# Raw weight loads behind the second pair's keys and queries, and one filler product per bank

## Chip, cores and metric

The kernel runs on one core of a Trainium2 chip. The metric is the device time of one execution in microseconds (us), as the median of several runs.

## What is computed

Causal attention with a decay per key (4 batches, 8 heads, 576 positions, head size 64), then a feed-forward layer with a maximum of three products, then a second one with a rational gate.

```python
def _attn_ref(q, k, v, f):
    scores = (1.0 / np.sqrt(D)) * np.matmul(q, k.transpose(0, 1, 3, 2))
    cum = np.cumsum(np.log(np.clip(f, 0.0001, 1.0)), axis=-1)
    scores = np.where(causal, -1e9, scores + cum[:, :, :, None] - cum[:, :, None, :])
    attn = softmax(scores)                       # row maximum subtracted
    return np.matmul(attn, v)

def _moe_ref(x, w1, w2, w3, w_out):              # 2304 x 512, d_ff 768
    h = np.maximum(np.maximum(x @ w1, x @ w2), x @ w3)
    return h @ w_out

def _moe2_ref(x, w_in, w_out, a, b):             # 2304 x 512, d_ff 2048
    h = x @ w_in
    P = a[0] + a[1]*h + a[2]*h**2 + a[3]*h**3
    Q = 1.0 + abs(b[0])*abs(h) + abs(b[1])*h**2
    return (P / (Q + 1e-6)) @ w_out
```

The weights of the two layers arrive as 64-bit floats; everything else is 32-bit.

## The kernel before

**Pairs, units and steps.** Attention works on pairs of heads (class Pair) and on units, one head of a pair with one group of query blocks (class Unit). Group 0 has the first 320 positions (three blocks), group 1 the other 256 (two blocks). The first batch comes as eight pairs: pairs 0 to 3 with group 0, pairs 4 to 7 with group 1. Later batches have both groups in one pair. A loop over steps (from L596) does, for three units at once, the last part of one (attend), the transposes of the next (turn), and the scores of a third, and prepares a pair some steps before its first unit.

**A pair's way.** load puts keys (kn) and queries (qn) into memory by three transfers each (L269, L272); both use a two-buffer tag, so a pair's loads wait for the transposes of the pair before. prepare transposes the keys on TensorE (L334) and copies them out on ScalarE (L308, tile kf), then fetches the decay rows of the keys by small transfers (copies, L57: kf<-nch for pair 0, from the tile nch; kf<-ncd for the others, from a copy in DRAM), then does the queries (L334, L320). scores multiplies both (L385, in the first batch two instructions on TensorE per product), VectorE adds the mask and finds the row maximum (L389), ScalarE takes the exponential (L395), GpSimd normalises (L404), TensorE transposes (L424), ScalarE copies out (L426), and attend multiplies with the values (L440).

**Fillers.** exercised (L80) issues WARM products of the tile warm, 128x512 in the fp32r type (L84), into a bank of PSUM before the bank's real work writes it. Their results are overwritten. It does so for pairs 0 to 3 (n < 4): at the transposes of keys and queries, the scores, the transposed probabilities and the outputs. That is 52 banks, so 104 fillers.

**Weights.** A 64-bit weight tile is loaded raw (load_raw, L167, 512 KB for w1 to w3) and converted into a high and a low 32-bit part: ScalarE (L181), VectorE (L186, L187, L188, L191), ScalarE (L197), GpSimd (L200). The list conv holds 30 such conversions: 18 of w1, w2 and w3, 12 of w_out. ahead holds the raw loads of the first three; each conversion begun later also issues one raw load further on. Two conversions are begun before the steps, the rest by fill, at 0.15 for each call before step 7 and 0.5 after it. Raw loads keep the order of the program among themselves and stand on the queue of SP, as all loads do.

**Order.** A planner orders the instructions of each engine ahead of the run, by its own estimates of their durations and of the program's order. On the chip each engine and SP's queue then work strictly in that order.

Of the kernel before, what the change touches and what calls it, by code (L numbers as in the profile page):

```python
# [37 lines left out]
def kernel(  # L38
# [17 lines left out]
    def move(dst, src):  # L56
        return nc.sync.dma_start(r32(dst), r32(src))  # L57
# [22 lines left out]
    def exercised(bank, n):  # L80

        if n < 4:
            for _ in range(WARM):
                nc.tensor.matmul(bank, warm[:, 0], wide, start=True, stop=True)  # L84
        return bank

    WARM = 2
    mask = const.tile([P, S], F32, name="mask")
    nc.gpsimd.memset(mask, 0.0)
    nc.gpsimd.affine_select(  # L90
# [424 lines left out]
    pairs = [Pair(n, *j) for n, j in enumerate(jobs)]  # L515
# [12 lines left out]
    ahead = [load_ for load_, _ in conv[: LOOK + 1]]  # L528
# [50 lines left out]
        return NCONV - int(state["c"])  # L579

    pairs[0].load()
    for load_ in ahead:
        load_()
    LV = 1
    lvat = {}
    for p in pairs[1:]:
# [2 lines left out]
        f_()  # L589
    move(ncd, nch)  # L590
    pairs[0].load_v()
    for _ in range(2):
        conv.pop(0)()
    pairs[1].load()
    ab = const.tile([P, 8], F32, name="ab")
    for step in range(len(slots) + 2):  # L596
        u = slots[step] if step < len(slots) else None
# [257 lines left out]
```

## Time and profile before

| | before |
|---|---|
| median of three runs | 959.67 us (959.0 to 960.5) |
| profiled execution | 959.34 us |
| its span, first to last instruction | 957.5 us |
| TensorE (PE) busy | 934.7 us (98%) |
| VectorE (DVE) | 725.0 us (76%) |
| ScalarE (ACT) | 641.3 us (67%) |
| GpSimd (POOL) | 252.0 us (26%) |
| mean granted clock of TensorE | 0.99 |

Busy times are of one profiled execution. PEld is TensorE's weight load, beside its products; SPq is the issue of a transfer on SP's queue. A matmul's recorded duration overlaps the next one's, so distances between starts, or the chain that ended last, tell what one costs in a stream. The granted clock is given as a share of full speed.

### The profile page before, as it was taken

To read this page: it belongs to the slowest core of one execution; us is meant where nothing else is said; L and a number is where in the kernel's file an instruction comes from. 1 tells how busy PE (TensorE), PEld (TensorE's weight loads), DVE (VectorE), ACT (ScalarE), POOL (GpSimd) and SP (SyncE) were. 2 spreads that over 40 slices of the span, in tenths; PEclk is the share of its full clock that TensorE was granted. 3 is DMA by queue.
4 is the path that set the end of the run, shared out by engine and by line. 5 is a ranking of instruction groups with operands and counts; after the bars stand their busy time and mean duration, and the time that the engine had idled before them with its cause. 6 is when DMAs were issued, how large, how long until landed. Compare 5 with 4: busy or idle time off the path is not lost.

```text
span 957.5 us, 16833 instructions
## 1 busy us (share of the span) xinstructions
PE 934.7 (98%) x5780; PEld 828.5 (87%) x5780; DVE 725.0 (76%) x1692; ACT 641.3 (67%) x1526; POOL 252.0 (26%) x408
## 2 busy tenths in 40 slices
PE   7989999999999999999999999999999999999998
PEld 5757899998998989999999988888888888899997
DVE  7578875556776786534297969888988988899996
ACT  6786667777767676656454558667666666777765
POOL 3355654444554465424132400000000000000000
PEclk9997999999999999999999999999999999999999
DMA  5784223123555455220145477011002102100000
GB/s 160 201 227 124 82 75 85 43 65 97 145 160 173 136 175 152 71 91 1 62 137 180 141 256 272 1 45 44 1 1 66 44 1 66 44 1 1 34 1 34
DMA packets 125741, 88.52 MB, mean 92 GB/s; under 512 B 74572, under 2 KB 110424, under 8 KB 125656
## 3 DMA queue, kind: packets, MB, share of 16 engines
q1 hardware_dynamic: 125656, 87.45, 30.5%
q8 instruction: 46, 0.75, 0.3%
q14 instruction: 39, 0.32, 0.1%
HBM read 64.73 MB, written 22.69 MB: 91 GB/s over the span
## 4 chain that ended last, share of the span: by engine, by line
PE 81%; DVE 12%; ACT 2%; issue 2%; DMA 2%; SPq 0%; POOL 0%; ACTq 0%; DVEq 0%; POOLq 0%
PE hq L730 7%; PE hq L728 7%; PE oo L778 7%; PE oo L779 7%; PE hq L729 7%; PE oo L777 7%; PE h L472 6%; PE h L473 5%; PE h L474 5%; PE o L440 5%; PE tp L424 5%; PE x2p L498 2%; PE s L388 2%; PE x2p L500 2%; PE s L387 2%
## 5 line engine op out<-in xcount | busy, mean ns | idle before, releaser
L472 PE MATMUL h<-x,w1h 128*128 128x320 f32 (+1 forms) x576 | 177.0, 308 | 2.0 <-DVE m L480 1.4
L474 PE MATMUL h<-x,w1l 128*128 128x320 f32 (+1 forms) x576 | 172.3, 299 | 0.0
L473 PE MATMUL h<-x,w1h 128*128 128x320 f32 (+1 forms) x576 | 172.2, 299 | 0.0
L404 POOL TENSOR_SCALAR e<-e,rs 128x64 f32<-128x64 f32 (+4 forms) x160 | 89.2, 573 | 104.3 <-DVE rs L401 90.7
L472 PEld LDWEIGHTS h<-x,w1h 128*128 128x128 f32 x576 | 109.7, 190 | 4.8 <-DVE m L480 1.6
L778 PE MATMUL oo<-wp,gh 128*128 128x512 f32 x288 | 112.6, 391 | 0.0
L777 PE MATMUL oo<-wp,gh 128*128 128x512 f32 x288 | 112.0, 389 | 0.0
L395 ACT ACTIVATE e<-e,st 128x64 f32<-128x64 f32 (+4 forms) x160 | 88.9, 556 | 32.1 <-DVE st L389 30.6
L473 PEld LDWEIGHTS h<-x,w1h 128*128 128x128 f32 x576 | 109.8, 191 | 0.4 <-ACT w1h L197 0.2
L737 ACT ACTIVATE s<-hq 128x512 f32<-128x512 f32 (+1 forms) x80 | 44.3, 554 | 97.6 <-PE hq L730 97.5
L474 PEld LDWEIGHTS h<-x,w1l 128*128 128x128 f32 x576 | 109.6, 190 | 0.0
L779 PE MATMUL oo<-wp,gl 128*128 128x512 f32 x288 | 109.1, 391 | 0.0
L389 DVE CUSTOM_DVE_ANT_0 e<-s,mask 128x320 f32<-128x320 f32 (+3 forms) x160 | 67.3, 432 | 37.2 <-PE s L388 27.3
L426 ACT ACTIVATE pt<-tp 128x384 f32<-128x384 f32 (+3 forms) x160 | 70.2, 470 | 21.5 <-PE tp L424 18.4
L740 DVE SCALAR_TENSOR_TENSOR s<-s,ab,u 128x512 f32<-128x512 f32 (+1 forms) x80 | 55.7, 696 | 32.3 <-ACT u L738 32.2
L424 PE MATMUL tp<-ident,e 128*128 128x128 f32 (+1 forms) x480 | 78.5, 279 | 1.5 <-DVE k2s L312 1.1
L730 PE MATMUL hq<-x,wil 128*128 128x512 f32 (+1 forms) x192 | 69.9, 364 | 0.0
L728 PE MATMUL hq<-x,wih 128*128 128x512 f32 (+1 forms) x192 | 69.8, 363 | 0.0
L729 PE MATMUL hq<-x,wih 128*128 128x512 f32 (+1 forms) x192 | 69.7, 363 | 0.0
L779 PEld LDWEIGHTS oo<-wp,gl 128*128 128x128 f32 x288 | 54.0, 188 | 11.3
L778 PEld LDWEIGHTS oo<-wp,gh 128*128 128x128 f32 x288 | 54.0, 188 | 10.5
L777 PEld LDWEIGHTS oo<-wp,gh 128*128 128x128 f32 x288 | 54.1, 188 | 10.4
(132 smaller groups left out, 2425.1 us busy)
## 6 DMA issues: line engine op xcount, KB each, us to landing
raw_w<-in_moe_w_dram SPq DMA_DIRECT2D x18, 512.0 KB
raw_wp<-in_moe_w_out_dram SPq DMA_DIRECT2D x32, 256.0 KB
wpd<-wp SPq DMA_DIRECT2D x32, 256.0 KB
raw_wi<-in_moe_w_in_dram SPq DMA_DIRECT2D x32, 256.0 KB
wp<-wpd SPq DMA_DIRECT2D x10, 768.0 KB
x2d<-xo SPq DMA_DIRECT2D x16, 320.0 KB
out_dram<-ob SPq DMA_DIRECT2D x18, 256.0 KB
kn<-in_k_dram SPq DMA_DIRECT2D x32, 128.0 KB
```

Source lines behind the costliest of these rows:

```text
L395: nc.scalar.activation(e[:nr], e[:nr], AF.Exp, bias=m, scale=-1.0, accum_out=l)
L404: nc.gpsimd.tensor_scalar(e, e, self.rs[:, 1, j : j + 1], 0.0, op0=ALU.mult, op1=ALU.add)
L424: nc.tensor.transpose(tp[:kr, dst : dst + P], self.e[i][:, Q0[c] : Q1[c]], ident)
L472: nc.tensor.matmul(hp_[:, :w], wh[:, j, dc], xs[dc][:, 1], start=(dc == NDC - 1), stop=False)
L473: nc.tensor.matmul(hp_[:, :w], wh[:, j, dc], xs[dc][:, 0], start=False, stop=False)
L474: nc.tensor.matmul(hp_[:, :w], wl[:, j, dc], xs[dc][:, 0], start=False, stop=(dc == 0))
L728: nc.tensor.matmul(hp_[:, :w], wih[:, dc, fs], xh, start=(dc == 0), stop=False)
L729: nc.tensor.matmul(hp_[:, :w], wih[:, dc, fs], xl, start=False, stop=False)
L730: nc.tensor.matmul(hp_[:, :w], wil[:, dc, fs], xh, start=False, stop=(dc == NDC - 1))
L777: nc.tensor.matmul(o, g[0][:, ts_], wh_, start=(fc == 0), stop=False)
L778: nc.tensor.matmul(o, g[0][:, ts_], wl_, start=False, stop=False)
L779: nc.tensor.matmul(o, g[1][:, ts_], wh_, start=False, stop=(fc == NF2 - 1))
```

## The change

Two edits. WARM goes from 2 to 1, so each of the 52 banks gets one filler. The raw loads in ahead, and the first two conversions with the raw load that they issue, stand in the program behind pair 0's values and behind pair 1's keys and queries; before, ahead stood directly behind pair 0's loads, and the two conversions ahead of pair 1's.

```diff
-    WARM = 2
+    WARM = 1
...
     pairs[0].load()
-    for load_ in ahead:
-        load_()
     LV = 1
...
     move(ncd, nch)
     pairs[0].load_v()
+    pairs[1].load()
+    for load_ in ahead:
+        load_()
     for _ in range(2):
         conv.pop(0)()
-    pairs[1].load()
     ab = const.tile([P, 8], F32, name="ab")
```

## Rows read from the trace of the kernel before

**Rows 1.** The page, part 1: busy time, share of the span, instructions of each engine.
```profile
PE 934.7 (98%) x5780; PEld 828.5 (87%) x5780; DVE 725.0 (76%) x1692; ACT 641.3 (67%) x1526; POOL 252.0 (26%) x408
```

**Rows 2.** Table of stages: from:to, length, busy us (instructions) per engine, clock, DMA.
```profile
22.00:49.00 27.00, 27.00 (x159) 21.37 (x158) 14.22 (x53) 21.19 (x65) 11.23 (x20) 1.00 0.70 189
49.00:55.00 6.00, 6.00 (x41) 4.53 (x39) 1.89 (x10) 5.80 (x21) 3.77 (x6) 1.00 0.33 76
60.00:68.00 8.00, 5.03 (x26) 2.44 (x25) 7.96 (x17) 7.61 (x19) 3.81 (x4) 1.00 1.17 301
68.00:82.00 14.00, 11.36 (x39) 8.30 (x38) 13.19 (x26) 10.39 (x24) 10.01 (x9) 0.51 0.63 179
108.00:300.00 192.00, 189.59 (x1470) 174.13 (x1467) 124.59 (x413) 138.74 (x412) 96.36 (x172) 1.00 0.37 101
```

**Rows 3.** The chain that ended last, 0 to 30 us: start, us, what.
```profile
6.62 5.09 DMA kf<-nch
12.27 4.18 DMA kn<-in_k_dram
23.86 0.47 PE s L84 x2
26.49 0.33 PE tk L334 x3
```

**Rows 4.** Timeline, 0 to 40 us: start, us, engine, line, operation, tiles, [idle before].
```profile
0.75 0.40 SPq L103 DMA_DIRECT2D fl<-in_f_dram  x1
3.19 0.45 DVE L108 TENSOR_SCALAR fl<-fl 32x576 f32<-32x576 f32 x1
4.22 1.57 SPq L167 DMA_DIRECT2D raw_w<-in_moe_w_dram  x3
5.75 1.20 PE L84 MATMUL tq<-warm 128*128 128x512 f32 x2
5.90 2.50 SPq L57 DMA_DIRECT2D kf<-nch  x4
10.16 0.56 PE L334 MATMUL tq<-ident,qn 128*128 128x128 f32 x3
11.70 0.47 SPq L167 DMA_DIRECT2D raw_w<-in_moe_w_dram  x1
11.84 0.79 PE L385 MATMUL s<-kf,qf 66*128 66x64 f32 x4 [0.65 <-DMA kf<-nch]
12.27 0.45 SPq L269 DMA_DIRECT2D kn<-in_k_dram  x1
15.33 1.10 SPq L57 DMA_DIRECT2D kf<-ncd  x2
22.03 0.71 PE L385 MATMUL s<-kf,qf 66*128 66x64 f32 x4
```

**Rows 5.** SP's waits, 0 to 20 us: line, releaser, total us, times, longest.
```profile
SPq L272 <- DMA raw_w<-in_moe_w_dram: 1.3, 1, 1.3
```

**Rows 6.** Table of stretches of 2 us, columns as in rows 2, GB/s last.
```profile
8.00:10.00 2.00, 2.00 (x6) 1.55 (x5) 1.09 (x3) 1.03 (x2) 0.00 (x0) 1.00 1.08 363
18.00:20.00 2.00, 2.00 (x6) 1.31 (x6) 1.59 (x7) 1.07 (x3) 0.46 (x1) 0.50 0.30 68
```

**Rows 7.** Groups of a conversion's steps, 22 to 49 us: busy us, mean ns, idle before.
```profile
L181 ACT ACTIVATE cv_w<-raw_w 128x512 f32<-128x512 f32 x4 | 2.4, 659 | 0.0
L197 ACT ACTIVATE w1h<-cv_w 128x512 fp32r<-128x512 f32 x5 | 3.1, 624 | 1.4 <-DVE cv_w L191 1.4
L188 DVE SCALAR_TENSOR_TENSOR cv_w<-raw_w,cv_w 128x512 int32<-128x512 int32 x4 | 2.6, 680 | 0.0
```

**Rows 8.** TensorE from 22 to 49 us: lines L84, L424 and L334, in this order.
```profile
22.00:49.00 27.00, 19.98 (x59) 9.64 (x58) 1.00 0.70 189
22.00:49.00 27.00, 5.11 (x31) 3.66 (x32) 1.00 0.70 189
22.00:49.00 27.00, 2.33 (x15) 1.95 (x15) 1.00 0.70 189
```

## The prediction, made before the changed kernel ran

> **What bounds the kernel now.** Read the page's engine shares first: TensorE is busy 934.7 of 957.5 us [rows 1]. Nearly everything after 108 us is a full TensorE (189.59 of 192 us up to 300 us), so a gain has to come from the first 100 us and reach the end as a shift. The table by stages then says what each early stage is worth [rows 2]. From 22 to 49 us TensorE is busy 27.00 of 27 us at granted clock 1.00, while ScalarE has 21.19 and VectorE 14.22. From 49 to 55 us ScalarE is full beside it (5.80 of 6). From 60 to 68 us VectorE is the full engine (7.96 of 8) and TensorE has only 5.03. At the very start the chain that ended last runs through two transfers: 5.09 us for the first pair's decay rows (kf<-nch) and 4.18 us for the second pair's keys [rows 3]. The timeline shows why: three raw weight tiles of 512 KB leave SP at 4.22, ahead of the four decay rows (5.90 to 8.40), and a fourth at 11.70, just ahead of those keys (12.27) [rows 4].
>
> My sum is made against the profiled execution, 959.34 us (span 957.5 and 1.84 around it). The median of the runs is 959.67, so 0.33 is added at the end.
>
> **Edit 1, the raw weights: the first pair.** Without them the decay rows have an empty ring. The nearest row for a transfer with nothing ahead of it is fl: issue ends at 1.15, its reader starts at 3.19, so 2.0 us [rows 4]. The first head's two rows have left SP by about 7.15, all four by 8.40: they land at 9.2 to 10.4 instead of 11.71. The queries must also be there: their transposes stand at 10.16, behind ten fillers that take 5.75 to 10.16, 0.44 us each. Half of those and one of the two ahead of the key transposes go, 2.6 us; so they start near 7.55. The first scores stand 1.1 us behind the last of these transposes (10.72 to 11.84), for the copy between. First scores: 7.55 + 0.56 + 1.1, about 9.2 for 11.84, 2.6 us earlier.
>
> **The second pair's keys.** Two things leave SP ahead of them: the fourth raw weight (0.57 us from 11.70 to 12.27), and a wait of 1.3 us for a raw weight that stood inside the first values' issue [rows 5]. They leave at about 10.7, and the first block is there at 10.7 + 0.4 + 2.0 = 13.1 instead of 16.45: 3.3 us earlier. TensorE, in order, waits for them in both versions.
>
> **What it moves into the way.** The four raw weights now stand on SP ahead of the second pair's decay rows (kf<-ncd, 15.33 now), and ahead of every later key, query and value load. SP reaches them near 13.7 (10.7 and six loads of 0.5 us). Upper bound: before, rows behind three such tiles landed 7.5 us after the first tile's issue (4.22 to 11.71); a fourth adds 0.5 MB at 363 GB/s [rows 6], 1.45 us, so 13.7 + 9.0 = 22.7. Lower bound: four tiles at 363 GB/s need 5.9 us, so about 20. The second pair's scores started at 22.03 [rows 4]. Everything else they need would be ready 5.0 us earlier, at 17.0 (3.3 from the keys, and five of the ten fillers between 16.5 and 22 us, 1.7 at 0.34 each, midway between 0.23 and 0.44). So the wait that left the keys comes back at these rows, and most of the gain with it. Gain at this point: between 5.0 (if the planner puts the rows ahead of the weights, or other TensorE work into the hole) and -0.7. I take 0.7, near the end given by the row that shows just such a queue.
>
> The conversions of these weights start some 10 us later. On VectorE a conversion has four steps, none over L188's 0.68 us [rows 7], so at most 2.7 us, and 10.9 for four; it has 12.8 us free from 22 to 49 [rows 2]: covered, unless the planner puts a conversion whose weight hasn't landed ahead of a score (rival 2). GpSimd has 15.8 us free there: covered too. ScalarE pays 0.66 + 0.62 us per conversion [rows 7]; about two of the four now fall behind 22 us: 2.6 us.
>
> **Edit 2, the fillers.** From 22 to 49 us 59 records of L84 stand on TensorE [rows 8]. A pair takes 0.47 us of the chain [rows 3], 0.23 each; 30 fewer are 6.8 us. If nothing else bounded, the stage would be 20.2 us. But ScalarE has 21.19 us of its own and receives 2.6: 23.8 us. So 27.0 - 23.8 = 3.2 us are gained. Bounds: 0, if the chain of score, exponential, normalisation and transpose leaves ScalarE as many holes as now, and 5.8, its whole idle time. I take 3.2, as ScalarE runs at 5.80 of 6 in the next stage, so it can be that full. From 49 to 60 us some fillers go too, beside a full ScalarE and VectorE: nothing.
>
> **The clock.** After the wait for the keys [rows 3] the granted clock is 0.50 at 18 to 20 us [rows 6], the lower of its two levels (1.2 GHz). The wait now comes a little later (13 to 21 us) with fewer fillers around it, so I expect the slow stretch to reach 2 to 3 us into the next stage: 0.7 us lost, bounds 0 and 2.
>
> **Behind 60 us** the work is the same and each stage waits for an engine that only starts earlier: 0, within 2 either way, since the planner orders each engine anew when its estimates shift.
>
> The sum: 0.7 + 3.2 - 0.7 = 3.2 us. 959.34 - 3.2 = 956.1 for the profiled run, 956.5 as a median.
>
> **A rule that speaks against edit 2.** In the stage in question 46 transposes (31 + 15) lie among the fillers [rows 8], three in 0.33 us [rows 3], and the clock stayed at 1.00. The Trainium skill ("TensorE: Matmul & The Clock Gate", Part 4: PE-mode transpose) says that transposes in that mode don't count as activity in the way that products do, and don't bring the full clock. By that rule the fillers are most of what holds the clock here, and halving them gives the first rival below, at its full length 972.4, rather than my sum. No row of this trace has transposes alone at length, so it isn't settled here.
>
> **Rival 1, the clock falls in the first batch (slower).** Of the 27 us, fillers are 13.6 (59 x 0.23), transposes 5.1 (46 x 0.11), the other products 8.3. After the change TensorE's work is 6.8 + 5.1 + 8.3 = 20.2 us at full clock; each microsecond at half clock does half of it. ScalarE's 23.8 hides up to 7.2 us of half clock; beyond 13.6 us of it the stage is longer than now, and at half clock throughout it takes 40.4 us, 13.4 more: 959.67 - 0.7 + 13.4 = 972.4. For it: 68 to 82 us, where after fillers end the clock is 0.51 over 14 us [rows 2]. Against it: that fall followed a stretch with TensorE at 5.03 of 8 us, and here 20.2 of 23.8 is expected, so the condition that the row shows isn't met. A part of it (14 to 20 us at half) gives 960 to 963. Chance of an end above 961.6: 0.15.
>
> **Rival 2, late weights stall an in-order engine (slower).** A conversion's first step on ScalarE, or its bits on VectorE, is ordered by the planner's estimate of landing. If each of the four lands 1 us after its place, the copies, exponentials and scores queued behind wait 1 us each, up to 4 us, while the second pair's rows land at 22.7: +0.7 + 4 - 3.2, so 961.2, and to 963 with a worse order behind 60 us. It decides once the stalls outweigh ScalarE's 3.2. Chance of an end above 961.6: 0.12.
>
> **Rival 3, no change.** The gain is there at 49 us and is swallowed: VectorE, full from 60 us with the conversions, has the late ones still to do. 958 to 961.5. Chance 0.20.
>
> **Rival 4, the wait at 22 us doesn't come.** The planner puts the rows ahead of the weights: 5.0 instead of 0.7, with ScalarE's 3.2 and the clock's 0.7: 952.2; with 5.8 for ScalarE and 2 behind 60 us, under 950. Chance 0.18.
>
> **How the numbers follow.** My forecast, 954 to 957.7, has 0.35 and is the likeliest; with rival 4 faster is 0.53. Same (within 0.2%, 1.9 us, about what a measurement of this kernel can tell from none) is 0.20. Slower is 0.15 + 0.12 = 0.27. Range: 951 leaves some 0.07 below; 965 takes in the partial clock fall and rival 2 and leaves about 0.1 above.
>
> **What would show it.** In the changed trace: first scores near 9.2; second keys' transposes near 13; the second pair's scores at 20 to 22, released by kf<-ncd; 30 or so L84 records in the stage that follows, with ScalarE above 0.9 of it and granted clock 1.00; the start of the full VectorE stretch 3 to 4 us earlier, and the same distance at the end. I am wrong if the second pair's scores start near 17, if the clock is 0.5 past 25 us, or if the early stages end earlier and the end doesn't move.

## The result, and the profile after

The changed kernel takes **966.17 us** (median; 965.59 to 967.1) beside 959.65 for the kernel before on the same chip: ratio 1.0066, 95% interval 1.0056 to 1.0076. It is slower by 6.5 us where 3.2 us were expected, and outside the range. The profiled execution took 965.59 us, with a span of 963.8.

The page's busy line, in the columns of [rows 1]: TensorE is busy 5.2 us less (52 fillers fewer) and its last instruction comes 6.3 us later.

```profile
PE 929.5 (96%) x5728; PEld 819.8 (85%) x5728; DVE 732.1 (76%) x1692; ACT 641.3 (67%) x1526; POOL 254.7 (26%) x408
```

The table of stages of the changed kernel answers to [rows 2]. From 22 to 49 us the clock is 0.81 and no engine is full; from 108 to 300 us TensorE stands idle 2.4 us more than before.

```profile
22.00:49.00 27.00, 23.50 (x108) 16.83 (x107) 18.57 (x56) 20.16 (x60) 14.21 (x18) 0.81 0.66 178
49.00:55.00 6.00, 5.31 (x32) 3.45 (x31) 4.89 (x16) 5.58 (x16) 2.78 (x5) 1.00 0.76 157
60.00:68.00 8.00, 5.77 (x37) 3.70 (x37) 7.90 (x16) 7.04 (x19) 5.25 (x5) 1.00 0.97 249
68.00:82.00 14.00, 9.73 (x40) 5.64 (x40) 12.77 (x27) 10.72 (x26) 9.57 (x10) 0.64 0.55 168
108.00:300.00 192.00, 187.18 (x1440) 172.51 (x1440) 126.31 (x406) 137.35 (x402) 97.19 (x172) 1.00 0.37 100
```

**The start went better than the sum said.** The changed kernel's timeline, beside [rows 4]:

```profile
5.57 0.62 SPq L57 DMA_DIRECT2D kf<-nch  x1
8.73 0.79 PE L385 MATMUL s<-kf,qf 66*128 66x64 f32 x4 [0.61 <-DMA kf<-nch]
9.40 0.39 SPq L269 DMA_DIRECT2D kn<-in_k_dram  x1
11.42 0.33 PE L334 MATMUL tk<-ident,kn 128*128 128x128 f32 x1 [0.40 <-DMA kn<-in_k_dram]
12.42 2.12 SPq L167 DMA_DIRECT2D raw_w<-in_moe_w_dram  x4
14.59 0.95 SPq L57 DMA_DIRECT2D kf<-ncd  x2
20.26 1.41 PE L440 MATMUL o<-pt,v 128*64 128x320 f32 x12
21.94 0.71 PE L385 MATMUL s<-kf,qf 66*128 66x64 f32 x4
```

The first scores start at 8.73 us (11.84 before), the second pair's key transposes at 11.42 (their wait before ended near 16.5). The second pair's scores stand where they stood, 21.94 for 22.03, but not for want of kf<-ncd: the planner put the whole first unit ahead of them, down to its product with the values (L440 at 20.26; in the kernel before at 31.27). The rows themselves landed at 21.1 and 21.4 us by the landing marks of the trace (17.5 and 17.7 before), inside the forecast 20 to 22.7. By the measure explained below, TensorE is some 7 us ahead at 22 us.

**Then the lead goes.** VectorE of the changed kernel from 21 to 31 us, with GpSimd's L200 and the TensorE rows that wait (the releaser in brackets):

```profile
21.27 1.58 POOL L200 TENSOR_TENSOR w1l<-cv_w,w1h 128x512 fp32r<-128x512 f32 x1 [3.48 <-ACT w1h L197]
21.64 1.50 DVE L187 TENSOR_SCALAR cv_w<-cv_w 128x512 int32<-128x512 int32 x1
23.07 0.41 DVE L186 TENSOR_SCALAR cv_w<-cv_w 128x512 f32<-128x512 f32 x1
23.40 0.68 DVE L191 SCALAR_TENSOR_TENSOR cv_w<-raw_w,cv_w 128x512 int32<-128x512 int32 x1
24.00 0.21 DVE L389 CUSTOM_DVE_ANT_0 e<-s,mask 128x64 f32<-128x64 f32 x1
24.28 0.50 PE L84 MATMUL s<-warm 128*128 128x512 f32 x1 [0.51 <-DVE st L389]
24.82 1.27 POOL L200 TENSOR_TENSOR w1l<-cv_w,w1h 128x512 fp32r<-128x512 f32 x1 [1.97 <-ACT w1h L197]
25.15 1.23 DVE L187 TENSOR_SCALAR cv_w<-cv_w 128x512 int32<-128x512 int32 x1
26.30 0.34 DVE L389 CUSTOM_DVE_ANT_0 e<-s,mask 128x192 f32<-128x192 f32 x1
26.70 0.50 PE L84 MATMUL s<-warm 128*128 128x512 f32 x1 [0.92 <-DVE st L389]
```

Scores that start at 21.94 are done by 22.65, yet their row maximum (L389) runs at 24.00, behind three steps of conversions; the next products into that bank wait for it. The waits of TensorE from 10 to 60 us (line, releaser, total us, times, longest) put a number on it; in the kernel before, the same view has kn (1.8) and kf<-nch (0.6) and no wait for L389.

```profile
PE s L84 <- DVE st L389: 2.5, 3, 1.1
PE tp L84 <- ACT pt L426: 1.7, 2, 1.3
PE tq L334 <- DMA qn<-in_q_dram: 1.4, 2, 1.1
PE s L385 <- DVE st L389: 1.0, 1, 1.0
```

Behind these gaps the granted clock falls, as the changed kernel's stretches of 2 us show. It is 0.50 for 10.2 us, from 31.0 to 41.2 (before: 3.4 us from 17.1).

```profile
26.00:28.00 2.00, 1.23 (x5) 0.89 (x6) 2.00 (x7) 1.91 (x5) 0.10 (x2) 1.00 0.96 291
30.00:32.00 2.00, 1.39 (x5) 1.10 (x6) 2.00 (x9) 1.68 (x5) 0.41 (x1) 0.76 0.63 119
36.00:38.00 2.00, 1.63 (x8) 0.99 (x7) 0.74 (x3) 1.31 (x4) 2.00 (x3) 0.50 0.24 59
```

**A measure for the rest.** Busy shares don't say how far a kernel has come. So from each trace I summed the columns of TensorE's products outside the fillers (those in fp32 twice), and took, for a time of the kernel before, the time at which another kernel had done the same sum. The difference is called its *state*: minus is ahead. It stems from the one profiled run of each kernel; medians move with it within some 1.2 us, but the profiled runs of e5, e6 and e7 lie 1.4 to 1.5 us above their medians. Each median's ratio is to the kernel before on the same chip (959.64 to 959.89). All in us:

| kernel | 22 | 35 | 50 | 75 | 110 | 200 | end | median | ratio, interval |
|---|---|---|---|---|---|---|---|---|---|
| after | -6.7 | +0.2 | -1.1 | -3.6 | -0.7 | +1.3 | +6.3 | 966.17 | 1.0066 (1.0056 to 1.0076) |
| e1 fillers only | -0.9 | -1.9 | -4.9 | -5.2 | -4.5 | -4.2 | -3.5 | 956.96 | 0.9972 (0.9963 to 0.9981) |
| e2 raw weights only | -3.8 | +1.1 | +0.2 | -3.2 | -1.3 | -0.5 | +2.2 | 961.18 | 1.0019 (1.0009 to 1.0029) |
| e3 before, one filler less | -0.3 | -0.3 | -0.3 | -1.8 | -2.1 | -0.3 | +1.3 | 960.39 | 1.0007 (0.9997 to 1.0016) |
| e4 after, one filler more | -7.2 | +0.6 | -0.3 | -2.8 | +2.5 | +2.1 | +2.3 | 961.77 | 1.0022 (1.0013 to 1.0031) |
| e5 after, late order of e4 | -7.1 | +0.1 | -1.6 | -4.0 | -1.2 | +2.3 | +2.4 | 960.34 | 1.0006 (0.9996 to 1.0016) |
| e6 before's loads, late order of after | -1.1 | -2.0 | -3.8 | -5.0 | -1.1 | +0.9 | +7.1 | 964.94 | 1.0053 (1.0037 to 1.0069) |
| e7 later conversions | -6.2 | -3.4 | -5.6 | -6.5 | -2.9 | +1.3 | +8.7 | 966.46 | 1.0062 (1.0038 to 1.0086) |
| e8 fillers only, late order of before | -0.9 | -1.9 | -5.0 | -5.3 | -4.3 | -3.8 | -1.9 | 957.17 | 0.9969 (0.9958 to 0.9981) |
| e9 before, no fillers | -0.9 | -0.2 | -1.0 | -1.8 | +1.5 | +2.1 | +3.3 | 962.81 | 1.0032 (1.0021 to 1.0043) |
| e10 e7 with late order of e1 | -4.8 | -1.9 | -5.0 | -7.8 | -5.4 | -2.4 | -0.1 | 958.65 | 0.999 (0.9977 to 1.0004) |

The column for 75 us flatters every kernel: the kernel before is at half clock from 68.3 to 82.0 us, the changed kernel from 72.0 to 82.2. The same sum gives the changed kernel -0.1 at 60 us, +0.9 at 65 and -1.1 at 82, and from 35 to 70 us it is never more than 2.1 ahead. So the 3.2 us that were predicted for the end are not there at 110 us either (-0.7). From there it loses 2.0 us up to 200 us and 5.0 behind 200, where not one instruction of the program was changed. Two places carry those 5.0 (the state moves by 1.7 from 284 to 300 us and by 3.5 from 340 to 354). The stretches 284 to 296 and 340 to 380 us of the kernel before, and then of the changed kernel:

```profile
284.00:296.00 12.00, 11.64 (x85) 11.25 (x84) 8.91 (x34) 8.11 (x29) 4.09 (x7) 1.00 0.60 194
340.00:380.00 40.00, 39.50 (x299) 35.45 (x298) 28.53 (x91) 27.84 (x84) 22.07 (x38) 1.00 0.58 167
```
```profile
284.00:296.00 12.00, 10.06 (x74) 9.55 (x72) 9.73 (x34) 8.24 (x25) 6.07 (x10) 1.00 0.49 153
340.00:380.00 40.00, 38.37 (x277) 33.89 (x277) 26.38 (x85) 27.78 (x82) 19.64 (x34) 0.96 0.53 153
```

What is behind them: TensorE's waits in the changed kernel, in the first stretch and in the second. In the kernel before the longest single wait in either stretch is 0.2 us.

```profile
PE tp L424 <- POOL e L404: 1.7, 1, 1.7
```
```profile
PE s L387 <- DVE st L389: 1.5, 4, 0.6
```

Around 352 us the planner put the scores of two units one behind the other, where before it had put products of the second layer (x2p, L498) among them. TensorE waits for the row maxima, has 1.23 of 2 us, and the clock falls to 0.50 for 3.4 us from 355.3. A longer gap need not be followed by a fall: around the wait of 1.7 us near 290 us the clock stays at 1.00 (last line):

```profile
352.00:354.00 2.00, 1.23 (x6) 0.89 (x6) 1.97 (x11) 2.00 (x10) 0.00 (x0) 1.00 0.54 146
356.00:358.00 2.00, 2.00 (x11) 1.92 (x10) 2.00 (x10) 1.18 (x5) 1.53 (x4) 0.50 0.20 65
290.00:292.00 2.00, 0.93 (x6) 0.83 (x7) 1.48 (x7) 1.75 (x7) 1.71 (x3) 1.00 0.41 134
```

### The profile page after: what moved, and what is told of

The parts are those of the page before. It is cut to its first block, busy times and chain, and to the rows that moved or that the text cites. A ratio compares the mean times of both kernels' runs of the same rounds, so it can differ in the third digit from the quotient of the medians.

```text
span 963.8 us, 16733 instructions
## 1 busy us (share of the span) xinstructions
PE 929.5 (96%) x5728; PEld 819.8 (85%) x5728; DVE 732.1 (76%) x1692; ACT 641.3 (67%) x1526; POOL 254.7 (26%) x408
## 4 chain that ended last, share of the span: by engine, by line
PE 82%; DVE 8%; ACT 3%; DMA 3%; issue 2%; POOL 1%; SPq 0%; POOLq 0%; ACTq 0%; DVEq 0%
PE hq L728 7%; PE oo L778 7%; PE hq L730 7%; PE hq L729 7%; PE oo L779 7%; PE oo L777 7%; PE h L472 6%; PE h L474 6%; PE h L473 6%; PE o L440 5%; PE tp L424 5%; PE x2p L498 2%; PE x2p L500 2%; PE x2p L499 2%; PE s L388 2%
## 5 line engine op out<-in xcount | busy, mean ns | idle before, releaser
L404 POOL TENSOR_SCALAR e<-e,rs 128x64 f32<-128x64 f32 (+4 forms) x160 | 89.8, 576 | 95.7 <-DVE rs L401 88.0
L389 DVE CUSTOM_DVE_ANT_0 e<-s,mask 128x320 f32<-128x320 f32 (+3 forms) x160 | 67.4, 431 | 32.8 <-PE s L388 18.8
L426 ACT ACTIVATE pt<-tp 128x384 f32<-128x384 f32 (+3 forms) x160 | 69.6, 470 | 21.4 <-PE tp L424 19.1
L424 PE MATMUL tp<-ident,e 128*128 128x128 f32 (+1 forms) x480 | 78.9, 282 | 4.6 <-POOL e L404 3.3
L424 PEld LDWEIGHTS tp<-ident,e 128*128 128x128 f32 (+1 forms) x480 | 55.9, 134 | 11.1 <-POOL e L404 6.5
L777 PEld LDWEIGHTS oo<-wp,gh 128*128 128x128 f32 x288 | 54.1, 188 | 10.5
```

The costliest lines, as they stand in the source:

```text
L404: nc.gpsimd.tensor_scalar(e, e, self.rs[:, 1, j : j + 1], 0.0, op0=ALU.mult, op1=ALU.add)
L424: nc.tensor.transpose(tp[:kr, dst : dst + P], self.e[i][:, Q0[c] : Q1[c]], ident)
L777: nc.tensor.matmul(o, g[0][:, ts_], wh_, start=(fc == 0), stop=False)
```

## The experiments

Theory: the early edits cost nothing in the end; the planner, which orders each engine by estimates, answered them with a late order that is 5 to 7 us worse. Rivals: the raw weights' place itself costs the time; the missing fillers do, through the clock.

**e1, e2: each edit alone.** e1 is the kernel before with WARM 1, e2 the changed kernel with WARM 2.

```diff
-    WARM = 2
+    WARM = 1
```

> One filler per bank, raw weights where they were. If the fillers alone cost the time (TensorE's clock falls in the first batch without them), this is slower than before by 4 us or more and the granted clock is 0.50 for 10 us or more between 22 and 50 us. If the late weights cost it, this is within 2 us of before or faster: 956 to 961. If neither edit costs anything as such, but the planner's new order behind 100 us does, TensorE's products outside the fillers have, at 100 us, got as far as before within 2 us, and the end differs from that by up to 5 us.

> Raw weights behind the second pair's loads, two fillers per bank. If the late weights cost the time, this is near the changed kernel, 964 to 968, and the conversions crowd VectorE from 17 to 31 us as there. If the fillers cost it, 957 to 961, with the granted clock at 1.00 from 24 to 60 us. If it is the planner's order behind 100 us, the products at 100 us are within 2 us of before and the rest of the difference arises later.

From 22 to 49 us, e1 and then e2:

```profile
22.00:49.00 27.00, 25.07 (x147) 17.91 (x145) 15.41 (x60) 24.68 (x78) 14.34 (x24) 1.00 0.75 197
```
```profile
22.00:49.00 27.00, 26.21 (x145) 19.41 (x144) 21.12 (x59) 20.93 (x61) 17.04 (x21) 1.00 0.70 187
```

Half the fillers, alone, do from 22 to 49 us what the prediction said: ScalarE becomes the full engine (24.68 of 27 us) and the clock stays at 1.00. By 50 us 4.9 us are gained, and 3.5 stay at the end. Ahead of that stretch e1 pays with the clock: it is 0.50 for 10.2 us from 11.5 us (before: 3.4 us). The raw weights alone are 3.8 us ahead at 22 us and 1.1 behind at 35, at full clock (its first half clock comes at 77.1 us): so that lead is lost without the clock's help. VectorE is at 13.78 of 16 us from 16 to 32 there (8.43 before), but TensorE's waits from 10 to 60 us have none for L389 (the longest is 1.1 us, for qn): in e2 the row maxima aren't shown to be the cause. The medians of the two edits alone differ from that of before by -2.7 and +1.5; together they make +6.5. The effects don't add. e1 fell into the range given for the late weights as the cause, which e2 then denied: it is at 961.18, not at 964 to 968.

**e3, e4: one filler.** One product of 0.23 us less in the 52nd bank of the kernel before (-1 in the line below); one more there in the changed kernel.

```diff
-            for _ in range(WARM):
+            for _ in range(WARM + (1 if len(banks) == 52 else 0)):
```

> The kernel before, with one filler of 104 left out, in the last bank of the first batch (0.23 us of TensorE). The planner's order is the same as before up to about 60 us and another one behind that. If the planner's order behind the first batch is what moves the time, this lies 2 to 6 us from before in either direction, with the difference arising behind 100 us. If the edits themselves cost the time, it lies within 1 us of 959.7.

> The changed kernel with one filler more, in the last bank of the first batch (0.23 us). The order is that of the changed kernel up to about 55 us and another one behind that. If the planner's order behind the first batch made the loss, this lies 2 to 6 us from 966.2, most likely below it; the half clock at 355 us is gone. If the edits themselves made it, 965 to 967.5.

One filler *more* makes the changed kernel 4.4 us faster (961.77), though it is 2.5 us behind at 110 us. From there on it loses nothing (+2.5, +2.1, +2.3), and the half clock near 355 us is gone. e4 so bears the theory out. e3 doesn't: 2 to 6 us were expected, and one filler less moves the median of the kernel before by 0.7 us, within the measurement and inside the range given for the rival; its state wanders between -2.1 and +1.3. A new order can move the time by more than 4 us, then, but need not. A product of 0.23 us can't give 4.4 us; the order that follows from it can.

**e5, e6, e8: late orders moved over.** Two products put into one later bank, or none into the fourth pair's, leave the early order and change the plan. In the order in which the traces show TensorE's products, fillers aside, e5 is the changed kernel up to about 120 us and e4 from about 180; e6 is e1 up to about 40 us and the changed kernel from about 87; e8 is e1 up to about 94 and the kernel before from about 142.

```diff
-        if n < 4:
-            for _ in range(WARM):
+        if n < 4 or len(banks) == 99:
+            for _ in range(WARM if n < 4 else 2):
```

This is e5's; e8 has it with bank 77 on e1. e6 is the kernel before with

```diff
-            for _ in range(WARM):
+            for _ in range((1, 1, 1, 0)[n]):
```

> The changed kernel with two filler products more (0.46 us) in one later bank, the 99th, of a pair behind the first four. TensorE's order is meant to stay that of the changed kernel up to about 110 us and to become, from about 170 us on, the order that the run with one filler more in the 52nd bank had. Theory A (the loss behind 110 us belongs to the order that the planner chose for the later work): 959 to 961, with the state at 110 us as in the changed kernel (within 1 us of before) and no half clock near 355 us. Theory B (the two edits leave a debt by 110 us that is paid later whatever the order): 965 to 967.

> The kernel before with its loads where they were, and 1, 1, 1 and 0 fillers per bank for pairs 0 to 3. The early order is that of the run with half the fillers alone; from about 65 us on TensorE's order is that of the changed kernel. Theory A (the late order costs 5 to 7 us by itself): the lead of 4 to 5 us at 65 us is spent behind 110 us, and the end is at 960.5 to 962. Theory B (the late loss comes from the raw weights' place, which is unchanged here): the lead is kept, 955 to 957.

> The kernel before with one filler per bank in the first four pairs, and two more products in the 77th bank, of a later pair. Up to about 60 us the order is that of the run with half the fillers alone, from about 138 us on that of the kernel before. Theory A (the early gain and the late order add up): 4 to 5 us ahead at 110 us and at the end, 955 to 956. Theory B (the gain of half the fillers hangs on its own late order): 957 to 960.

e5 takes 5.8 us off the changed kernel by two useless products. e6, with its raw weights where they were, is at 964.94 instead of e1's 956.96. Both go the way of theory A; e6 is 3 us above my figure. Its lead was gone before the late order began: the fourth pair has no fillers, the clock is 0.50 from 44.8 to 55.0 us (first line below), and the state goes from -5.9 at 48 us to -1.5 at 55 and -1.5 at 82. From 110 us on it loses as the changed kernel does: 2.0 us up to 200 (both) and 6.2 behind it (5.0). Its rows show the losses in the same places:

```profile
49.00:55.00 6.00, 5.79 (x24) 3.39 (x23) 1.55 (x5) 4.75 (x15) 3.82 (x8) 0.50 0.69 175
284.00:296.00 12.00, 10.03 (x73) 9.54 (x72) 9.72 (x33) 8.60 (x25) 6.06 (x10) 1.00 0.47 148
340.00:380.00 40.00, 38.89 (x274) 34.60 (x273) 26.66 (x85) 28.54 (x84) 20.27 (x35) 0.91 0.54 153
```

and e5 has neither:

```profile
284.00:296.00 12.00, 11.59 (x85) 10.92 (x83) 9.71 (x36) 9.36 (x30) 7.83 (x14) 1.00 0.55 160
340.00:380.00 40.00, 39.85 (x309) 36.50 (x308) 28.63 (x91) 27.86 (x81) 19.87 (x37) 1.00 0.60 169
```

e8 comes to 957.17, 1 us above the range that I gave for theory A and at the lower edge of theory B's; it tells little more than that e1's gain doesn't hang on its own late order. From 200 us to the end, kernels that share an order move alike: after +5.0 and e6 +6.2; e4 +0.2 and e5 +0.1; before 0 and e8 +1.9; e1 +0.7, e9 +1.2 and e10 +2.3.

**e7, e10: conversions later.** e7 is the changed kernel without the two conversions ahead of the steps; e10 adds two products in the 70th bank, and from about 195 us has e1's order.

```diff
-    NCONV = len(conv) - 2
+    NCONV = len(conv)
...
-    for _ in range(2):
-        conv.pop(0)()
```

> The changed kernel without the two conversions that are begun ahead of the steps; all conversions are begun by the calls in the steps, so none stands among the first pairs' scores. Theory A (the lead of 7 us at 22 us is lost because the conversions crowd VectorE in front of the scores from 17 to 31 us): VectorE below 11 of 16 us from 16 to 32 us (14.5 in the changed kernel), and a lead of 3 to 5 us still there at 45 us. Theory B (it is lost at the transfers that stand behind the raw weights, or by the fall of the clock for want of fillers): no lead at 45 us, TensorE waiting for keys, queries or decay rows. The end holds a late order of its own, 3 to 7 us either way, and isn't the test.

> The kernel with the late conversions (raw weights late, one filler, no conversion ahead of the steps) and two more products in the 70th bank, of a later pair. Up to about 75 us the order is that of the run with the late conversions, from about 205 us on that of the run with half the fillers alone. Theory A (its lead of 5.6 us at 50 us was there, and its end was lost in the late order): 2 to 4 us ahead at 110 us and at the end 956 to 959. Theory B (raw weights that come late cost the time behind 110 us themselves, since the conversions end later): 963 to 967 again.

In e7 the lead of 6.2 us at 22 us is still 4.3 at 45 and 5.6 at 50; the changed kernel has 0.1 and 1.1 there. Its waits for L389 from 10 to 60 us fall from 3.5 us to 1.0:

```profile
PE s L84 <- DVE st L389: 0.7, 1, 0.7
PE s L385 <- DVE st L389: 0.3, 1, 0.3
```

VectorE, though, has 13.15 of 16 us from 16 to 32, not under 11: four conversions still run in that stretch, one or so fewer than in the changed kernel. So it isn't VectorE's sum that decides. That it is where the conversions stand among the scores is likely but not shown: e7 also has another order of TensorE's products from about 19 us, and its half clock in this stage is shorter, 6.8 us from 29.9 (10.2 from 31.0). e7's end (966.46) has a late loss of its own, which e10 takes away: 958.65, with 5.4 us of lead at 110 us. Raw weights that come late don't, then, cost the time by themselves. But 5.3 us of e10's lead are still lost behind 110 us, and it isn't better than e1.

**e9: no fillers.** The kernel before with WARM 0.

> The kernel before with no filler product at all, its loads where they were. What is asked is how much of the first batch's full clock the fillers carry. Theory A (the transposes and the other products carry it, as the run with half the fillers had 1.00 from 22 to 49 us): clock above 0.9 from 22 to 49 us, ScalarE about 25 of 27 us there as with half the fillers, 4 to 6 us ahead at 50 us. Theory B (without the fillers the transposes leave TensorE at half clock, the Trainium skill's rule on them in TensorE: Matmul & The Clock Gate, Part 4): clock 0.5 for 15 us or more of these 27, and no lead, or one under 2 us, at 50 us. From about 200 us on the order is that of the run with half the fillers alone.

```profile
16.00:32.00 16.00, 13.41 (x46) 9.70 (x47) 8.09 (x29) 12.31 (x38) 8.73 (x12) 1.00 0.54 139
22.00:49.00 27.00, 21.51 (x104) 14.89 (x103) 15.37 (x54) 20.70 (x66) 13.54 (x20) 0.90 0.67 183
44.00:48.00 4.00, 0.64 (x2) 0.13 (x1) 4.00 (x8) 2.41 (x11) 3.43 (x3) 0.50 0.76 202
```

The clock column misleads here. It prints 1.00 up to 43.3 us, but the products don't run at that pace. Three transposes (L334) take 0.85 us at 30.18, as they do at 48.86, where the granted clock is 0.50; at 37.75 they take 0.49:

```profile
30.18 0.85 PE L334 MATMUL tq<-ident,qn 128*128 128x128 f32 x3
37.75 0.49 PE L334 MATMUL tq<-ident,qn 128*128 128x128 f32 x3
48.86 0.85 PE L334 MATMUL tk<-ident,kn 128*128 128x128 f32 x3
```

By such distances e9 runs at the lower level from its start to about 33 us, and at the full one only from there to 43.3 us. Then the granted clock is 0.50 for 13.7 us. So about 17 of the 27 us from 22 to 49 are at the lower level, ScalarE has 20.70 of them, and 1.0 us of lead is there at 50 us: theory B's signs, not theory A's. From 44.6 to 48.2 us TensorE also stands still (0.64 of 4 us from 44 to 48) behind a normalisation on GpSimd (its longest wait for L404 is 3.5 us), and a lead of 4.7 us at 45 goes with it. The median is 962.81, slower than before: the second filler was waste, the first is not.

## Why the prediction was wrong, point by point

- **The start** was right: first scores forecast near 9.2, measured 8.73; second keys near 13, measured 11.42, since SP had the gap for the first values too.
- **The wait at 22 us** (gain 0.7 instead of 5.0) was wrong as a mechanism. I held the order of TensorE's work fixed and asked which input would be late. The rows landed when I had said, but the planner filled the hole with the first unit, and the gain at 22 us was 6.7. That is rival 4's result by another way than the one it names (the rows left SP at 14.59, behind the weights), and by 33 us the gain was gone.
- **"Covered"** is the step that failed first. I set 10.9 us of conversions against 12.8 us of free VectorE time in 27 us. They came in one go from 17.4 us, at 14.51 of 16 us from 16 to 32, ahead of the row maxima on an engine that works in order. Rival 2 named the place and about the price (four waits near 1 us); the conversions ran once their weights had landed, so it was their planned place ahead of the row maxima, not a late weight, that made these waits. I had also taken each step at no more than 0.68 us: L187 took 1.23 and 1.50 beside L200. Even in the kernel before L188 has a mean of 1.40 us from 16 to 32 us, ahead of the stretch of [rows 7].
- **The fillers** (3.2 us, ScalarE as the bound at 23.8) were right for the edit alone: 24.68 and 4.9 us in e1. With both edits there was no ScalarE bound to reach: it has 20.16 of 27 us, TensorE 23.50 at a clock of 0.81.
- **The clock** was forecast at 0.7 us, 2 to 3 us of half clock in this stage; it was 10.2. Rival 1's condition, gaps on TensorE beforehand, was met after all: 11.34 of 16 us from 16 to 32. It is also one of the signs of being wrong that I had named (0.5 past 25 us). Neither edit alone shows it from 22 to 49 us; e4, e5 and e7, which have both edits, do (6.8, 10.2 and 6.8 us). At 50 us the changed kernel is only 1.3 us ahead of e2: of e1's 4.9 us from the fillers, 3.6 aren't to be had there. How much of these is the clock's and how much the waits', no run parts. An estimate from the trace: TensorE is busy 9.54 us of the 10.2 at half clock, work of about 4.8 us at full clock, so the clock cost up to 4.8 us; the waits for L389 add up to 3.5.
- **"Behind 60 us: 0, within 2 either way"** is the step that gave the sign. The state is -0.1 at 60 us and -0.7 at 110, and +6.3 at the end: 7.0 us are lost behind 110 us, in work that the diff doesn't touch. I had written that the planner orders each engine anew and then priced it at 2; the runs' own spread, from 110 us to the end, is -0.2 (e4) to +8.2 (e6) and +11.6 (e7). Of the 9.7 us between forecast and result, these 7.0 are the greater part; the other 2.5 are the early gain, 3.2 forecast and 0.7 there at 110 us.
- **The rule on transposes** (the Trainium skill, "TensorE: Matmul & The Clock Gate", Part 4: PE-mode transpose) did not decide. By it transposes don't count as activity as products do. With one filler per bank e1 has 1.00 from 22 to 49 us, against the length that rival 1 took from the rule. Without any, e9 runs at the lower level until about 33 us, on transposes, scores and outputs, which goes the rule's way. Since the scores stand among the transposes and TensorE also waited (13.41 of 16 us from 16 to 32), no run here has transposes by themselves, and the rule itself stays open.
- **Small slips** without effect: by its own terms the second keys leave at 10.4 (12.27 - 0.57 - 1.3), not 10.7; and 14 to 20 us at half clock give 959 to 962, not 960 to 963.

What stays open: why exactly this plan puts two units' scores together near 352 us, and which estimate tips it. That the order, and not the loads or the fillers, carries the loss behind 200 us is shown by e5 and e6. From 110 to 200 us it is open: e6 loses the same 2.0 us in the same order, but e5 loses 3.5 there, mostly in another. And the loss of the early lead, by conversions ahead of row maxima and by the clock, is read from the traces; no run has one of the two alone.

## What to carry to other kernels

Where a planner orders every engine, an early edit is two changes: what it does, and a new plan for all that follows. Give that plan a price of its own, from a change so small that it can do nothing else (one filler less moved the time by 0.7 us, one more by 4.4), before the edit is blamed or praised; a plan can be moved back with a product or two. A lead is to be read at more than one time: the changed kernel's -3.6 us at 75 us stood between -0.1 at 60 and -1.1 at 82. And idle time of an in-order engine covers new work only where that work stands behind what others wait for: 12.8 free microseconds on VectorE did not hide 10.9.

Of all kernels measured, the best is the second edit alone: e1 with 956.96 us, 0.9972 of before, and e8, not to be told from it, with 957.17 and 0.9969.

## What the runs showed of the hardware

**VectorE beside GpSimd.** L187 takes 0.42 us alone (20.12 us in the changed kernel). Issued while L200 runs on GpSimd it took 1.50 and 1.23 us, and it ended 0.29 us behind L200's end both times (23.14 and 22.85; 26.38 and 26.09), as if it had waited the whole of L200 out. The Trainium skill ("SBUF — State Buffer", Summary: rules for kernel authors) says that of the two engines the second to issue is blocked until the first has finished, where VectorE is in a mode that uses two ports, or reads two operands from SBUF while GpSimd reads it too. The times of these two agree with such a block; L187 reads one tile, and whether it runs in that mode no trace here tells. L187 so cost 0.8 and 1.1 us more than by itself.

**Half the clock by a plan.** At 352 us, in the middle of steady work, 0.77 us of waiting in 2 us stood ahead of 3.4 us at 0.50; in e6, with the same order, the clock is 0.50 for 6.8 us from 352.0. e7, with an order of its own, has 3.4 us from 354.1; kernels with other orders there (e1, e4, e5, e8 to e10) stay at 1.00. Since 0.93 of 2 us at 290 us had no fall behind it, what tips it isn't shown.

**A printed clock of 1.00 isn't yet full pace.** At the start of each trace the column reads 1.00, and the products run at half of it. In the kernel before the fillers up to 10.16 us stand 0.43 us apart, and 0.23 later; the column has 1.00 from 8 to 10 us [rows 6]. In e9 this lasts until about 33 us. So early in a kernel the distance between products decides, not the column.
